# Fifteen of eighteen 128x1024 tiles transposed by a DMA of 16-bit halves instead of matmuls with the identity

## The chip, the cores and the metric

The kernel runs on one core of one Trainium2 chip. The metric is the device time of one execution in microseconds (us), the median of the runs shown. The engines are TensorE (PE), VectorE (DVE), ScalarE (ACT), GpSimd (POOL) and SyncE (SP), which issues all DMAs of this kernel.

## What is computed

An attention block and two feed-forward blocks, on 2304 tokens, in 32-bit floating point. Only the last block is touched by the change:

```python
def _moe2_ref(x, w_in, w_out, g_ln):
    h = x @ w_in                                   # 2304x512 @ 512x1024
    h_max = np.max(h, axis=-1, keepdims=True)
    e = np.exp(h - h_max)
    sm = e / (np.sum(e, axis=-1, keepdims=True) + 1e-09)
    solu = h * sm
    mu = np.mean(solu, axis=-1, keepdims=True)
    var = np.mean((solu - mu) ** 2, axis=-1, keepdims=True)
    ln = (solu - mu) / np.sqrt(var + 1e-06) * g_ln
    return (ln @ w_out).astype(np.float32)         # 2304x1024 @ 1024x512
```

## The kernel before

The kernel is one long program; a scheduler fixes, when it is built, the order of the instructions on each engine. Each engine then works its own queue strictly in that order and waits on semaphores for what other engines and DMAs deliver. Every matmul is done in three passes: an operand is split into a high part (`hi`, L92, a rounding copy on ACT) and a low part (`lo`, L98, a subtraction on DVE), and high x high, high x low and low x high are summed.

The stages before (attention, first feed-forward block, the product of two weight matrices) are left as they are. The last stage runs over 18 tiles of 128 tokens (`NT = 18`, L579) in the loop at L799. One turn of the loop issues, for tile t:

- `h_unit(t)` (L692): 24 matmuls into a PSUM tile `h` of 128x1024; then on DVE a row maximum (L708), on ACT `exp` into `e` (L710), on DVE sum, reciprocal and product into `so` (L711 to L714), the mean (L717), on ACT the squares (L718, written into `e` again), on DVE, POOL and DVE the variance, its power -1/2 and the normalised tile `so` (L719 to L723).
- `x2_unit` (L665), twice with one 128-row part each: 24 matmuls each for the input of the chunk of 256 tokens after this one; each part is evicted and split by ACT and DVE (`x2h`, `x2l`, L94 and L99).
- `tr2(t-1)` (L730): the normalised tile of the turn before, 128 tokens x 1024 features, is turned to features x tokens by 8 matmuls with the identity (L738), into two PSUM tiles; ACT rounds each half into `lh` (L94), DVE subtracts into `ll` (L99).
- `out_unit(t-2)` (L744): 24 matmuls `o` with `lh` and `ll` as stationary operands, an eviction on ACT (L754), and the DMA of 256 KB to the output (L755).
- `split_g` (L652), every second turn: `hi` and `lo` of 8 pieces of the next chunk's input (`gh`, `gl`).

Two lines of pools matter for the change. `e` has a single buffer, and so has the output tile `o`:

```python
e = p2.tile([128, DF], F32, tag="e", bufs=1, name="e")
o = p2.tile([128, DM], F32, tag="o", bufs=1, name="o")
```

`lh`, `ll`, `so` and the PSUM tile `h` have two buffers each.

Of the kernel before, what the change touches and what calls it, by code (L numbers as in the profile page):

```python
# [8 lines left out]
F32 = mybir.dt.float32  # L9
F32R = mybir.dt.float32r  # L10
U32 = mybir.dt.uint32
AF = mybir.ActivationFunctionType
ALU = mybir.AluOpType
AX = mybir.AxisListType
# [11 lines left out]
def tile_attention_moe(  # L26
# [15 lines left out]
    nc = tc.nc  # L42
    B, H, D, _, S = qkT.shape
    NH = B * H
    T, DM = out.shape
    w1, w2, w3L, wo1, w_in, wo2 = (w.bitcast(U32) for w in (w1, w2, w3L, wo1, w_in, wo2))
    DF = w_in.shape[1] // 2
# [38 lines left out]
    def smalltile(name):  # L86
        return PSP[1].tile([128, 512], F32, tag="B", name=name)

    def flat(ap):
        return ap.rearrange("p a b -> p (a b)")  # L90

    def hi(dst, src, eng=None):  # L92
        if eng is None:
            nc.scalar.activation(out=dst, in_=src, func=AF.Copy)  # L94
        else:
            eng.tensor_copy(out=dst, in_=src)

    def lo(dst, src, hi_, eng=nc.vector):  # L98
        eng.tensor_tensor(out=dst, in0=src, in1=hi_.bitcast(F32), op=ALU.subtract)  # L99
# [80 lines left out]
    def softmax_tile(h, ti, ps_in, cut=None):  # L180
# [8 lines left out]
        else:  # L189
# [5 lines left out]
        ex = nc.scalar.activation(  # L195
            out=dst, in_=dst, func=AF.Exp, bias=st[0:rows, ti:ti + 1], scale=-1.0,
            accum_out=st[0:rows, 5 + ti:6 + ti],
# [24 lines left out]
    def normalise(h):  # L222
# [3 lines left out]
        for ti, (q0, rows, n, o) in enumerate(QT):  # L226
            dst = p_t[h][0:rows, o:o + n]
            r = st[0:rows, 10 + ti:11 + ti]
            if ti < 2:
                nc.scalar.activation(out=dst, in_=dst, func=AF.Copy, scale=r)  # L230
            else:
# [83 lines left out]
    def ab_unit(n, f, half):  # L315
# [18 lines left out]
        def a():  # L334
            ps = mm(W1H, W1L, "a")
            a_sb = r0.tile([128, HS], F32, tag="a_sb", bufs=2, name="a_sb")
            nc.scalar.activation(out=a_sb, in_=ps, func=AF.Copy)  # L337
            st["a"] = a_sb
# [18 lines left out]
    def to_f32(raw, eng=nc.gpsimd, dst=None):  # L357

        low, high = raw[:, :, 0], raw[:, :, 1]
        if eng is None:  # L360
            nc.scalar.activation(out=high.bitcast(F32), in_=high.bitcast(F32), func=AF.Copy, scale=2.0 ** -112)
        else:
# [7 lines left out]
        )  # L370
        res = low if dst is None else dst.bitcast(U32)
        nc.vector.scalar_tensor_tensor(
# [23 lines left out]
    def stage(src):  # L396
        raw = stg[0].tile([128, CW, 2], U32, tag="stage", bufs=stg[1], name="stage")
        dst = flat(raw)
        if len(src.shape) == 3:
            dst = dst.rearrange("p (c f) -> p c f", c=src.shape[1])  # L400
        if after[0] is None:
            nc.sync.dma_start(out=dst, in_=src)
        else:
            with tc.issue_after(after[0].ins):
                nc.sync.dma_start(out=dst, in_=src)
        return raw
# [29 lines left out]
    def spill_job(i):  # L436
        src = w_in[i // 2 * 128:i // 2 * 128 + 128, i % 2 * 1024:i % 2 * 1024 + 1024] if i < 8 else wo2[(i - 8) * 128:(i - 7) * 128]

        def conv(raw):
            t = at.tile([128, CW], F32, tag="cst", bufs=2, name="cst")  # L440
            to_f32(raw, None, t)
            if i >= 8:
                nc.scalar.activation(out=t, in_=t, func=AF.Copy, scale=gln[:, i - 8:i - 7])
            nc.sync.dma_start(out=wf_scr[i], in_=t)
# [30 lines left out]
    for i in range(2):  # L475
# [16 lines left out]
        out=wmask[:, S - 128:S], in_=wmask[:, S - 128:S], pattern=[[-1, 128]],  # L492
# [27 lines left out]
    for st, (h, ph) in enumerate(steps):  # L520
# [33 lines left out]
        if h is not None:  # L554
            if h % 2 == 1:
                load_v(h // 2)
            if NQ - 2 <= h < NQ:
                t = QK[h % 2] = at.tile([128, 4, S], F32R, tag="QK", bufs=2, name=f"QK{h % 2}")
# [20 lines left out]
    NT = T // 128  # L579
# [148 lines left out]
    lt_t = {}  # L728

    def tr2(t):  # L730
        so = ln_t.pop(t)
        LH = p2.tile([128, KF, 128], F32R, tag="lh", bufs=2, name="lh")
        LL = p2.tile([128, KF, 128], F32R, tag="ll", bufs=2, name="ll")
        for hf in range(2):
            ps = smalltile("tr2")
            for k in range(4):
                c = hf * 4 + k
                nc.tensor.transpose(ps[:, k * 128:k * 128 + 128], so[:, c * 128:c * 128 + 128], ident)  # L738
            sl = slice(hf * 4, hf * 4 + 4)
            hi(flat(LH[:, sl]), ps)  # L740
            lo(flat(LL[:, sl]), ps, flat(LH[:, sl]))
        lt_t[t] = (LH, LL)

    def out_unit(t):  # L744
        LH, LL = lt_t.pop(t)
        ps = smalltile("o")
        for k in range(KF):
            for l_, w_ in ((LH, OH), (LH, OL), (LL, OH)):
                nc.tensor.matmul(  # L749
                    ps, l_[:, k], w_[:, k],  # L750
                    start=(k == 0 and l_ is LH and w_ is OH), stop=(k == KF - 1 and l_ is LL),
                )
        o = p2.tile([128, DM], F32, tag="o", bufs=1, name="o")
        nc.scalar.activation(out=o, in_=ps, func=AF.Copy)  # L754
        nc.sync.dma_start(out=out[t * 128:t * 128 + 128], in_=o)  # L755
# [32 lines left out]
    p2 = ctx.enter_context(tc.tile_pool(name="p2", bufs=1, side="left"))  # L788
# [10 lines left out]
    for t in range(NT + 2):  # L799
        c, o = divmod(t, 2)  # L800
        if t < NT:
            h_unit(t)
        if t < NT and c + 1 < NCH and 2 * t >= EX:
            x2_unit(c + 1, 2 * o)
        if 0 <= t - 1 < NT - 1:
            tr2(t - 1)
        if t < NT and c + 1 < NCH and 2 * t + 1 >= EX:
            x2_unit(c + 1, 2 * o + 1)
        if t < 2:
            for k in range(4):  # L810
                wf_split(8 + 4 * t + k, V)
        if 0 <= t - 2 < NT:
            out_unit(t - 2)
        if t == NT:
            tr2(t - 1)
        if t < NT and c + 2 < NCH:
            split_g(c + 2, o)
            if o == 1 and c + 3 < NCH:
                load_g(c + 3)
# [50 lines left out]
```

## Time and profile before

| | |
|---|---|
| median of 3 runs (lowest to highest) | 763.17 us (762.51 to 764.19) |
| the profiled execution's own time | 763.22 us |
| its span, first to last instruction | 761.4 us |
| PE busy | 744.4 us (98%), 4864 matmuls |
| PE share of the chain that ended last | 78%, of it the tile transposes (L738) 2% |
| DVE / ACT / POOL busy | 454.9 / 405.9 / 90.6 us |
| mean granted clock of TensorE | 0.995 |

The profile lists busy time per engine over the span, the chain of work that ended last (followed back from the last instruction, each step to what released it), groups of instructions with their mean durations, and waits. In the last stage the names are: `h`, `x`, `o` the three products, `tr` the transposes. The buffer numbers of tiles are left out in the profile's rows.

### The profile page before, as it was taken

How to read it: one execution, taken by the hardware profiler on the slowest of the kernel's cores; microseconds unless marked ns; L12 is line 12 of the kernel's file. 1: busy time of each engine (PE TensorE's matmuls, PEld its weight loads, DVE VectorE, ACT ScalarE, POOL GpSimd, SP SyncE). 2: the span in 40 equal slices, each digit the busy share in tenths (PEclk: the TensorE clock that was granted, in tenths of full speed). 3: DMA queues.
4: the chain of work that ended last, by engine and by line, in shares of the span. 5: the costliest groups of instructions: out<-in, count | busy, mean ns of one | idle time of the engine just before them, and what ended most of it. 6: DMA issues, size and time to landing. Idle time of an engine off the chain costs nothing.

```text
span 761.4 us, 13032 instructions
## 1 busy us (share of the span) xinstructions
PE 744.4 (98%) x4864; PEld 649.6 (85%) x4864; DVE 454.9 (60%) x1165; ACT 405.9 (53%) x927; POOL 90.6 (12%) x93
## 2 busy tenths in 40 slices
PE   8989998999999999999999999999999999999997
PEld 6567978878988988999998898888888888888885
DVE  7877878898777767427868846443435343433341
ACT  4987878898867778415536534332334243222232
POOL 5033313223222121000000000000000000000000
PEclk9999999999999999999999999999999999999999
DMA  4643645566765553106659612221202000000001
GB/s 111 176 121 97 188 134 163 177 171 202 198 173 178 178 161 105 60 32 230 219 163 341 239 56 56 69 53 31 70 15 70 15 15 15 14 15 15 15 28 41
DMA packets 44242, 83.97 MB, mean 110 GB/s; under 512 B 7370, under 2 KB 18634, under 8 KB 44180
## 3 DMA queue, kind: packets, MB, share of 16 engines
q1 hardware_dynamic: 44180, 83.15, 35.8%
q8 instruction: 38, 0.62, 0.3%
q14 instruction: 24, 0.20, 0.1%
HBM read 57.47 MB, written 18.57 MB: 100 GB/s over the span
## 4 chain that ended last, share of the span: by engine, by line
PE 78%; ACT 0%; DVE 0%; issue 0%; ACTq 0%; DVEq 0%
PE o L749 13%; PE x L680 13%; PE h L700 13%; PE b L325 11%; PE a L325 11%; PE m L602 6%; PE av L297 3%; PE tr L264 2%; PE tr L738 2%; PE sc L177 2%; PE sc L178 1%; PE tr L266 0%; PE tr L273 0%; ACT o L754 0%; ACT lh L94 0%; DVE g_sb L345 0%
## 5 line engine op out<-in xcount | busy, mean ns | idle before, releaser
L195 ACT ACTIVATE P<-P,STAT 128x576 f32<-128x576 f32 (+4 forms) x160 | 88.2, 553 | 35.0 <-DVE STAT L191 34.4
L708 DVE TENSOR_REDUCE sv<-h 128x1 f32<-128x1024 f32 x18 | 22.1, 1225 | 119.5 <-PE h L700 119.5
L99 POOL TENSOR_TENSOR QK<-qk,QK 64x1152 fp32r<-64x1152 f32 x24 | 66.5, 2774 | 169.5 <-ACT QK L94 169.3
L680 PE MATMUL x<-gh,MH 128*128 128x256 f32 x288 | 81.7, 284 | 0.0
L680 PE MATMUL x<-gl,MH 128*128 128x256 f32 x288 | 80.5, 279 | 0.0
L680 PE MATMUL x<-gh,ML 128*128 128x256 f32 x288 | 80.4, 279 | 0.0
L191 DVE CUSTOM_DVE_ANT_0 P<-sc,wmask 128x576 f32<-128x576 f32 (+4 forms) x160 | 70.7, 479 | 7.3 <-PE sc L169 5.3
L722 POOL TENSOR_TENSOR sv<-sv,mhalf 128x1 f32<-128x1 f32 x18 | 9.9, 548 | 444.1 <-DVE sv L719 444.1
L325 PE MATMUL b<-xT0h,W 128*128 128x288 f32 x256 | 57.3, 299 | 1.5 <-DVE STAT L191 0.8
L325 PE MATMUL a<-xT0h,W 128*128 128x288 f32 x256 | 57.9, 299 | 0.7 <-ACT a_sb L337 0.7
L749 PE MATMUL o<-OH,lh 128*128 128x512 f32 x144 | 57.1, 397 | 0.3 <-ACT lh L94 0.3
L325 PE MATMUL a<-xT1h,W 128*128 128x288 f32 x256 | 57.2, 298 | 0.0
L749 PE MATMUL o<-OH,ll 128*128 128x512 f32 x144 | 57.0, 396 | 0.0
L749 PE MATMUL o<-OL,lh 128*128 128x512 f32 x144 | 56.8, 395 | 0.0
L700 PE MATMUL h<-IH,x2l 128*128 128x512 f32 x144 | 56.6, 393 | 0.0
L700 PE MATMUL h<-IL,x2h 128*128 128x512 f32 x144 | 56.5, 392 | 0.0
L325 PE MATMUL b<-xT1h,W 128*128 128x288 f32 x256 | 56.5, 294 | 0.0
L700 PE MATMUL h<-IH,x2h 128*128 128x512 f32 x144 | 56.2, 390 | 0.0
L710 ACT ACTIVATE e<-h,sv 128x1024 f32<-128x1024 f32 x18 | 20.1, 1117 | 66.5 <-DVE sv L708 65.1
L680 PEld LDWEIGHTS x<-gl,MH 128*128 128x128 f32 x288 | 54.2, 188 | 1.2
L754 ACT ACTIVATE o<-o 128x512 f32<-128x512 f32 x18 | 10.8, 598 | 83.1 <-PE o L749 83.1
L680 PEld LDWEIGHTS x<-gh,MH 128*128 128x128 f32 x288 | 54.2, 188 | 0.9
(124 smaller groups left out, 1922.4 us busy)
## 6 DMA issues: line engine op xcount, KB each, us to landing
stage<-in_w_dram SPq DMA_DIRECT2D x32, 512.0 KB
g_scr<-g_sb SPq DMA_DIRECT2D x32, 288.0 KB
stage<-in_wo_dram SPq DMA_DIRECT2D x16, 512.0 KB
qk<-in_qk_dram SPq DMA_DIRECT2D x24, 288.0 KB
QK<-QK SPq DMA_DIRECT2D x24, 288.0 KB
graw<-g_scr SPq DMA_DIRECT2D x6, 1024.0 KB
out_dram<-o SPq DMA_DIRECT2D x18, 256.0 KB
VT<-in_vm_dram SPq DMA_DIRECT2D x16, 256.0 KB
```

What stands on the lines that cost most here:

```text
L99: eng.tensor_tensor(out=dst, in0=src, in1=hi_.bitcast(F32), op=ALU.subtract)
L177: nc.tensor.matmul(view, t[:, 0, q0:q0 + rows], t[:, 3, c0:c0 + w], start=True, stop=False)
L191: mx = nc.vector.tensor_tensor_reduce(out=dst2, in0=ps_in, in1=msk, scale=-SCALE, scalar=BIG, op0=ALU.add, op1=ALU.min, accum_out=st[0:row ...
L195: ex = nc.scalar.activation(out=dst, in_=dst, func=AF.Exp, bias=st[0:rows, ti:ti + 1], scale=-1.0, accum_out=st[0:rows, 5 + ti:6 + ti],)
L297: nc.tensor.matmul(st["ps"][64 * e:64 * e + 64, 448 + c0:448 + c1], vr[:, j, e], PT[(2 * p + e) % 4][:, o + c0:o + c1], **kw,)
L325: nc.tensor.matmul(ps, w_[:, c, fs], x_[:, c, sl], start=(c == 0 and w_ is WH and x_ is XH), stop=(c == KC - 1 and w_ is WL),)
L602: nc.tensor.matmul(ps, w_[:, k % 4], o_[:, k], start=(k == 0 and w_ is H3 and o_ is WOH), stop=(k == KF - 1 and w_ is L3),)
L680: nc.tensor.matmul(ps[m], w_[:, k, m * 128:m * 128 + 128], g_[:, k], start=(k == 0 and w_ is MH and g_ is GH), stop=(k == KF - 1 and w_ is ...
L700: nc.tensor.matmul(ps[:, hf], x_[:, k, ts_], w_[:, k, hf * 512:hf * 512 + 512], start=(k == 0 and x_ is XH and w_ is IH), stop=(k == KC - ...
L708: nc.vector.reduce_max(out=sv[:, 0:1], in_=psf, axis=AX.X, negate=True)
L710: nc.scalar.activation(out=e, in_=psf, func=AF.Exp, bias=sv[:, 0:1], scale=1.0, accum_out=sv[:, 1:2])
L749: nc.tensor.matmul(ps, l_[:, k], w_[:, k], start=(k == 0 and l_ is LH and w_ is OH), stop=(k == KF - 1 and l_ is LL),)
```

## The change

For tiles 0 to 14 (`t < NT - 3`), `tr2` uses no matmul. ACT copies the tile, seen as 16-bit halves, so that the 1024 low halves of a row stand first and its 1024 high halves behind (`half`, 128x2048 of 16 bits). One DMA on SP's queue transposes its 16 blocks of 128x128 (`turned`, 512 KB). DVE copies the halves back together (`lt`, 128x1024 of 32 bits). Then `hi` and `lo` make `lh` and `ll` from `lt`, in SBUF, and not from PSUM. `half` takes the one buffer of `e` (`tag="e"`); `turned` and `lt` have one buffer each. Tiles 15 to 17 take the old path.

```diff
+U16 = mybir.dt.uint16
...
         LL = p2.tile([128, KF, 128], F32R, tag="ll", bufs=2, name="ll")
+        if t < NT - 3:
+            half = p2.tile([128, 2, DF], U16, tag="e", bufs=1, name="half")
+            turned = p2.tile([128, 2, DF], U16, tag="turned", bufs=1, name="turned")
+            lt = p2.tile([128, DF], F32, tag="lt", bufs=1, name="lt")
+            nc.scalar.copy(out=half, in_=so.bitcast(U16).rearrange("p (f w) -> p w f", w=2))
+            nc.sync.dma_start_transpose(
+                out=turned.rearrange("p w (k t) -> p (w k) t", t=128), in_=half.rearrange("p w f -> p (w f)"),
+            )
+            nc.vector.tensor_copy(out=lt.bitcast(U16).rearrange("p (f w) -> p w f", w=2), in_=turned)
+            for hf in range(2):
+                sl = slice(hf * 4, hf * 4 + 4)
+                src = lt[:, hf * 512:hf * 512 + 512]
+                hi(flat(LH[:, sl]), src)
+                lo(flat(LL[:, sl]), src, flat(LH[:, sl]))
+            lt_t[t] = (LH, LL)
+            return
         for hf in range(2):
             ps = smalltile("tr2")
```

In the changed file, lines up to L730 of before are one higher, and lines from L734 on are 17 higher: `exp` is L711 there, the eviction of `o` L771, `hi` L95, `lo` L100. The new copy on ACT is L739, the DMA L740, the copy on DVE L743.

The queues up to the last stage are as before. In the last stage they change at these two places.

ACT, before, one turn of the loop for an even tile, past the middle of the stage (`lh<-tr2` is `hi` of the transposed tile, `e<-so` the squares):

```order
L754 ACTIVATE o_6872<-o_6847 128x512
L710 ACTIVATE e_6908,sv_6906<-h_6881,sv_6906 128x1024
L94 ACTIVATE x2h_6775<-x2_6919 128x256
L94 ACTIVATE lh_6946<-tr2_6948 128x512
L94 ACTIVATE lh_6946<-tr2_6955 128x512
L718 ACTIVATE e_6908,sv_6906<-so_6912,sv_6906 128x1024
L94 ACTIVATE x2h_6775<-x2_6962 128x256
```

ACT with the change, in the same part of the stage (`half<-so` is the new copy; `so_7150` is the tile before `so_7286`):

```order
L771 ACTIVATE o_7248<-o_7223 128x512
L95 ACTIVATE lh_7184<-lt_7188 128x512 x2
L711 ACTIVATE e_7282,sv_7280<-h_7255,sv_7280 128x1024
L95 ACTIVATE x2h_7293<-x2_7295 128x256
L719 ACTIVATE e_7282,sv_7280<-so_7286,sv_7280 128x1024
L95 ACTIVATE x2h_7293<-x2_7334 128x256
L739 COPY half_7324<-so_7150 128x2048
L771 ACTIVATE o_7386<-o_7361 128x512
L95 ACTIVATE lh_7322<-lt_7326 128x512 x2
L711 ACTIVATE e_7416,sv_7414<-h_7389,sv_7414 128x1024
```

The two `hi` of a tile stood between `exp` and the squares of the next; now the copy of that tile stands behind the squares and the second `x2h`, and its two `hi` stand in front of the `exp` of the tile after next, which also takes over the buffer that the DMA reads (in turns with `split_g`, four `gh` stand in front of the copy).

DVE, before, the same turns (`ll<-tr` is `lo` of the transposed tile):

```order
L723 TENSOR_SCALAR so<-so,sv 128x1024
L708 TENSOR_REDUCE sv<-h 128x1
L711 TENSOR_SCALAR sv<-sv 128x1
L712 RECIPROCAL sv<-sv 128x1
L714 SCALAR_TENSOR_TENSOR so,sv<-h,sv,e 128x1024
L99 TENSOR_TENSOR x2l<-x_7205,x2h 128x256
L99 TENSOR_TENSOR ll<-tr_7234,lh 128x512
L99 TENSOR_TENSOR ll<-tr_7241,lh 128x512
L717 TENSOR_SCALAR sv<-sv 128x1
```

DVE with the change:

```order
L715 SCALAR_TENSOR_TENSOR so,sv<-h,sv,e 128x1024
L100 TENSOR_TENSOR x2l<-x_7295,x2h 128x256
L718 TENSOR_SCALAR sv<-sv 128x1
L720 TENSOR_SCALAR sv<-sv 128x1
L100 TENSOR_TENSOR x2l<-x_7334,x2h 128x256
L724 TENSOR_SCALAR so<-so,sv 128x1024
L743 COPY lt<-turned 128x2x1024
L100 TENSOR_TENSOR ll<-lt,lh 128x512 x2
L709 TENSOR_REDUCE sv<-h 128x1
```

The two `lo` stood between the product (L714) and the mean (L717); now the joining copy and both `lo` stand in front of the row maximum of the next `h` (in turns with `split_g`, four `gl` stand in front of the joining copy, and the row maximum comes between the two `lo`).

On PE a turn was `h` (24 matmuls, with the 24 of one `x` part, the 8 transposes and the 24 of the other `x` part put in before its last 6) and `o`; it is now `o`, `h`, `x`, `x`. On SP the transposing DMA of a tile stands in front of the output DMA of the tile before.

## Rows read from the trace of the kernel before

**Rows 1.** The page: span, busy time by engine, the chain by engine.

```profile
span 761.4 us, 13032 instructions
PE 744.4 (98%) x4864; PEld 649.6 (85%) x4864; DVE 454.9 (60%) x1165; ACT 405.9 (53%) x927; POOL 90.6 (12%) x93
PE 78%; ACT 0%; DVE 0%; issue 0%; ACTq 0%; DVEq 0%
```

**Rows 2.** Busy time by stretch (length; PE, PEld, DVE, ACT, POOL; clock, DMA share, GB/s).

```profile
600.00:650.00 50.00, 50.00 (x302) 44.26 (x301) 22.28 (x44) 17.93 (x34) 1.64 (x3) 1.00 0.05 17
```

**Rows 3.** The chain in order of time, last stage (start, length, what).

```profile
482.96 0.87 PE tr L738 x8
...
593.53 5.59 PE o L749 x24
599.12 4.13 PE h L700 x18
...
606.07 0.87 PE tr L738 x8
606.94 2.81 PE x L680 x24
609.75 1.38 PE h L700 x6
611.13 5.59 PE o L749 x24
```

**Rows 4.** Timeline of DVE, one turn (start, length, instruction, wait before it).

```profile
603.30 1.23 DVE L708 TENSOR_REDUCE sv<-h 128x1 f32<-128x1024 f32 x1 [8.67 <-PE h L700]
...
606.26 1.28 DVE L714 SCALAR_TENSOR_TENSOR so<-h,sv,e 128x1024 f32<-128x1024 f32 x1
...
607.47 0.42 DVE L99 TENSOR_TENSOR x2l<-x,x2h 128x256 fp32r<-128x256 f32 x1
607.81 1.28 DVE L99 TENSOR_TENSOR ll<-tr,lh 128x512 fp32r<-128x512 f32 x2
609.01 0.15 DVE L717 TENSOR_SCALAR sv<-sv 128x1 f32<-128x1 f32 x1
```

**Rows 5.** Timeline of ACT, the same turn.

```profile
604.64 1.11 ACT L710 ACTIVATE e<-h,sv 128x1024 f32<-128x1024 f32 x1 [4.88 <-DVE sv L708]
...
606.54 1.09 ACT L94 ACTIVATE lh<-tr 128x512 fp32r<-128x512 f32 x2
609.25 1.15 ACT L718 ACTIVATE e<-so,sv 128x1024 f32<-128x1024 f32 x1 [1.62 <-DVE sv L717]
...
610.39 0.36 ACT L94 ACTIVATE x2h<-x 128x256 fp32r<-128x256 f32 x1
610.66 2.18 ACT L94 ACTIVATE gh<-graw 128x512 fp32r<-128x512 f32 x4
```

**Rows 6.** ACT copies in SBUF: tile QK (min/median/max ns); groups by shape, 540 to 720 us.

```profile
L94 ACT ACTIVATE QK<-qk x24: 1160/1164/1176, 46.2 to 287.2; 64x1152 fp32r<-64x1152 f32 x24
...
L94 ACT ACTIVATE gh<-graw 128x512 fp32r<-128x512 f32 x16 | 8.7, 619 | 0.0
```

**Rows 7.** DVE, one source: groups by shape, 540 to 720 us; timeline at 348 us.

```profile
L708 DVE TENSOR_REDUCE sv<-h 128x1 f32<-128x1024 f32 x10 | 12.3, 1225 | 77.1 <-PE h L700 77.1
...
L723 DVE TENSOR_SCALAR so<-so,sv 128x1024 f32<-128x1024 f32 x11 | 8.9, 812 | 2.1 <-POOL sv L722 2.1
...
348.85 0.43 DVE L367 TENSOR_SCALAR stage<-stage 128x512 uint32<-128x512 uint32 x1 [2.73 <-DMA stage<-in_wo_dram]
```

**Rows 8.** The last output DMA: its issue in the timeline, and SP's wait for it.

```profile
758.47 0.33 SPq L755 DMA_DIRECT2D out_dram<-o  x1
...
SPq L865 <- DMA out_dram<-o: 1.6, 1, 1.6
```

**Rows 9.** The page: bytes moved in 40 slices; DMA queue (packets, MB, share of 16 engines).

```profile
GB/s 111 176 121 97 188 134 163 177 171 202 198 173 178 178 161 105 60 32 230 219 163 341 239 56 56 69 53 31 70 15 70 15 15 15 14 15 15 15 28 41
...
q1 hardware_dynamic: 44180, 83.15, 35.8%
```

## The prediction

> **What bounds the kernel now.** I read the page first: PE is busy for 744.4 of 761.4 us, and of the chain that ended last 78% is PE and nearly nothing is any other engine [rows 1]. An average over stages can hide another limit, so next the busy time by stretch: from 600 to 650 us PE has 50.00 of 50 us at full granted clock, DVE 22.28, ACT 17.93, and the DMA engines 5% [rows 2]. Then the chain in order of time: in the last stage it is PE alone, without a gap, and one turn of the loop is six pieces in a row, 593.53 to 611.13, 17.60 us [rows 3]. The 8 transposes of a tile are one of these pieces, 0.87 us, the same from the first to the last. The chain charges only the distance to the next matmul, so 0.87 us is the price on the path; the longer busy time that a group shows overlaps its neighbours and is not to be used.
>
> So every transposed tile taken off PE is worth 0.87 us, as long as PE still gets its operands in time. The question is whether the longer way round through ACT, DMA and DVE stays hidden beneath a turn that is then 17.60 - 0.87 = 16.73 us.
>
> **What is removed.** 15 tiles x 0.87 = 13.05 us of PE. The `hi` and `lo` of the tile remain, at 0.55 us (1.09 for two) and 0.64 us (1.28 for two) each [rows 4, 5]; I take the same from SBUF.
>
> **What is added, per tile.** Three pieces, none of which the trace of before shows.
>
> - The copy `half` on ACT, 2048 elements a row. ACT copies in SBUF took 1.164 us for 1152 elements and 0.619 for 512 [rows 6]: 0.85 ns an element, so 1.164 + 896 x 0.85 ns = 1.93 us. Below it stands 1.11, the `exp` of as many bytes [rows 5]; above it double the slope for the split access, about 3.7. I take 1.93, since the engine's other rows go by elements.
> - The joining copy on DVE, also 2048 elements. One-source work in SBUF took 0.812 us for 1024 and 0.43 for 512 [rows 7]: 0.75 ns an element, so 0.812 + 1024 x 0.75 ns = 1.58, taken as 1.6. Bounds: 0.81 (as many bytes) and 2.45 (twice the row maximum's 1.225, the slowest rate in the stage).
> - The DMA, D. The output DMA of 256 KB landed 0.33 + 1.6 = 1.9 us after SP began to issue it [rows 8]. 512 KB take 0.77 us more at the best slice's 341 GB/s [rows 9]: 2.7 us is the lower bound. Two such DMAs one after the other would be 3.9. The far bound: a row of a 128-wide block of 16-bit elements is 256 bytes, 2048 such pieces, 128 for each of 16 engines; the kernel's mean packet costs 0.358 x 16 x 761.4 us / 44180 = 99 ns [rows 1, 9], so 12.6 us of packets behind a start of about 1.2 (1.9 less the data's 0.77): 13.8 us. That mean is over packets of 1.9 KB, so the value belongs near the lower end; I take 3.5.
>
> As pure load this fits: 3.5 us more on ACT and DVE together for each turn, against 27.7 and 32.1 us idle in 50 [rows 2]; the DMA queue is nearly empty here. PSUM traffic falls.
>
> **The round that the new order closes.** What decides is not load but a ring of waits. With the change DVE takes the row maximum of tile n+1 only behind the joining copy and `lo` of tile n-1, and ACT takes `exp` of n+1 behind the two `hi` of n-1 and only once the DMA has read `half`, because both share one buffer. The DMA of n-1 in turn waits for `half`, which stands behind the squares of tile n. So one round leads from row maximum to row maximum, and its length must be under a PE turn. From the timelines, counted from 603.30 [rows 4, 5]:
>
> - row maximum to the end of the product: 606.26 + 1.28 - 603.30 = 4.24; `x2l` ends at 607.89, 4.59. Before, the two `lo` came here (607.81 to 609.01); now the mean follows directly, 0.15, and the squares 0.24 after its start: 4.83. From the squares to the second `x2h` is 610.39 - 609.25 = 1.14, and 0.27 more until ACT is free: 6.24 us.
> - in every second turn four `gh`, 2.18.
> - `half` 1.93, DMA 3.5, join 1.6, one `hi` 0.55, one `lo` 0.64, and a second `lo`, 0.64, in turns without `gh`; five handoffs between engines at 0.1 (the row maximum ends at 604.53, `exp` starts at 604.64), 0.5.
>
> Without `gh`: 6.24 + 1.93 + 3.5 + 1.6 + 0.55 + 1.28 + 0.5 = 15.60. With `gh`: 6.24 + 2.18 + 1.93 + 3.5 + 1.6 + 0.55 + 0.64 + 0.5 = 17.14. Mean 16.37, against 16.73 of PE: 0.36 us to spare. A single late turn is caught by PE's own slack: the last `x2l` is wanted only after the next `o`, some 4 us later than it is ready. Write S for the sum of the three new pieces, 7.03 here. Up to S = 7.4 PE never waits; beyond it each round is longer by S - 7.4, in about 14 rounds (tiles 1 to 14).
>
> For `o` the way is free too: tile n-1 is complete about 15 us after the row maximum of n began, and its `o` stands behind two `x`, one `o`, one `h` and two more `x`, 22 us. On SP each transposing DMA waits for its `half`; behind it stands an output DMA whose data comes later anyway, so that costs nothing. The tail (tiles 15 to 17) keeps its order: nothing.
>
> **Sum.** The profiled execution took 763.22 us, the median is 763.17, the same. 763.2 - 13.05 = 750.2 us.
>
> **The rivals.**
>
> 1. *The forecast:* S at most 7.4, all 13.05 us gained, 750.2. For it: all three middle estimates. Against it: the margin is 0.4 us on three prices that no row shows. Chance 0.55.
> 2. *Part of it is given back:* S between 7.4 and 8.2, for instance a join at 2.45, S = 7.88, a loss of 14 x 0.48 = 6.7 us: 756.9. Chance 0.19. The no-change strip around S = 8.33 (13.05 / 14 = 0.93 over 7.4) gets 0.04.
> 3. *Slower: the ring becomes the bound.* Place: the row maximum on DVE and `exp` on ACT wait for the transposing DMA of the tile before the last. The point that decides is S = 8.33, that is D = 4.8 with the other two as taken. At D = 6, S = 9.53 and the loss 14 x 2.13 = 29.8: 780 us. For it: the far bound of the DMA lies well beyond, and the loss is steep, 14 us for each us. Against it: the output DMA's 1.9 us. Chance 0.20, of it 0.07 up to D = 5.5 (14 x 1.63 = 22.8, 773).
> 4. *The 16 blocks go one after another:* if each paid a DMA's start of 1.2 us, D = 16 x 1.2 + 1.5 of data = 20.7, S = 24.2, a loss of 14 x 16.8 = 235: 985 us. Chance 0.02. Against it: 256 KB in 128 rows did not pay any such thing in the output DMA [rows 8]. Beside it, the Trainium skill's page "VectorE: DVE Perf Modes", section "The three transpose paths", gives 1309 ns for a 128x128 transpose of 16-bit elements by DMA against 390 ns on TensorE, and advises TensorE when the result may go to PSUM. By that price, paid 16 times in a row, the sum would come to some 989 us. No run here shows a transposing DMA yet.
>
> That the change does not do what it says is excluded by the order of the instructions: 15 transposing DMAs stand on SP, and three groups of 8 transposes are left on PE.
>
> **Range and chances.** About 0.2%, 1.5 us, is what a measurement of this kernel can tell from no change. From 749 (the forecast with its spread) to 773 (D = 5.5) the cases hold 0.55 + 0.19 + 0.04 + 0.07 = 0.85; the rest lies above. Faster 0.55 + 0.19 = 0.74, same 0.04, slower 0.22. The forecast's own range is 749 to 752.
>
> **What would show it.** Right: a turn of 16.7 us in the chain, `o`, `h`, `x`, `x` without gaps, PE still about 50 of 50 us between 600 and 650, `half` near 1.9 us, the join near 1.6, and the join starting about 3.5 us after `half` ends. Wrong: gaps on PE before `h` or `o`; DVE idle in front of the join with the DMA as releaser, for over 5 us, and `exp` waiting likewise; then the turn equals the ring and not PE's work. If the turn is 16.7 us and the time is still not near 750, the loss lies at the start or the end of the stage, which I cost at nothing.

## The result and the profile after

| | before | after |
|---|---|---|
| median (lowest to highest) | 763.68 us (762.51 to 764.78, 4 runs) | 751.07 us (750.47 to 753.42, 4 runs) |
| ratio to before, 95% interval | | 0.9841 [0.9814, 0.9868] |
| profiled execution, its span | 763.22, 761.4 us | 750.76, 749.0 us |

The kernel is faster by 12.6 us, against a forecast of 13.05. The page of the kernel after answers to [rows 1, 9]: PE lost 120 matmuls and 13.6 us of busy time, DVE gained 20.6 us and ACT 26.4 us, and the DMA moved 31,200 packets more, all of them under 512 bytes (38,570 now, 7,370 before). The last row is the new joining copy. In the chain by engine 10% are now DMA, of it 4% the transposing one and 4% a load of an earlier stage.

```profile
PE 730.8 (98%) x4744; PEld 636.1 (85%) x4744; DVE 475.5 (63%) x1180; ACT 432.3 (58%) x942; POOL 90.6 (12%) x93
DMA packets 75441, 91.82 MB, mean 123 GB/s; under 512 B 38570, under 2 KB 49834, under 8 KB 75380
PE 72%; DMA 10%; DVE 10%; ACT 5%; issue 1%; POOL 1%; ACTq 0%; SPq 0%; DVEq 0%; POOLq 0%
L743 DVE COPY lt<-turned 128x2048 uint16<-128x2048 uint16 x15 | 20.2, 1344 | 60.5 <-DMA turned<-half 60.5
```

Busy time by stretch answers to [rows 2] (length; PE, PEld, DVE, ACT, POOL; clock, DMA share, GB/s). From 600 us on PE is as full as before. In the two stretches ahead of that it is not: 0.76 and 0.15 us are idle.

```profile
500.00:550.00 50.00, 49.24 (x276) 42.16 (x276) 24.70 (x46) 22.72 (x37) 1.65 (x3) 1.00 0.37 95
550.00:600.00 50.00, 49.85 (x286) 43.38 (x285) 26.24 (x46) 23.26 (x37) 1.65 (x3) 1.00 0.27 69
600.00:650.00 50.00, 50.00 (x289) 43.80 (x289) 26.72 (x49) 24.62 (x41) 1.65 (x3) 1.00 0.18 48
```

The chain in order of time, late in the stage, answers to [rows 3]. From `o` to `o` a turn is 652.62 - 635.94 = 16.68 us (16.73 was forecast), without a gap.

```profile
635.94 5.59 PE o L766 x24
641.52 5.50 PE h L701 x24
647.02 5.60 PE x L681 x48
652.62 5.59 PE o L766 x24
```

The new pieces can be read from the timelines of the same turn, that of ACT here and that of DVE below it (start, length, instruction, wait before it). The copy `half` takes 1.89 us and ends at 640.56. The joining copy starts at 644.38, and its releaser is the DMA: 3.82 us from the end of one to the start of the other. The join takes 1.33 us. One `hi` and one `lo` from SBUF take 0.62 and 0.69 us, nearly as from PSUM before (0.60 and 0.68).

```profile
638.67 1.89 ACT L739 COPY half<-so 128x2048 uint16<-128x2048 uint16 x1
```

The timeline of DVE, the same turn:

```profile
644.38 1.33 DVE L743 COPY lt<-turned 128x2048 uint16<-128x2048 uint16 x1 [3.82 <-DMA turned<-half]
```

What was not foreseen stands early in the stage. There the chain runs through the transposing DMA, which takes twice as long in some tiles:

```profile
493.24 5.33 DMA turned<-half
...
508.83 6.87 DMA turned<-half
...
524.98 3.68 DMA turned<-half
...
542.61 7.46 DMA turned<-half
...
550.10 1.37 DVE lt L743
...
551.49 0.64 ACT lh L95
```

SP's timeline shows what sets the long ones of 6.9 to 7.5 us apart. In these, SP has issued the load of the next chunk's input (`graw`, up to 1 MB) right in front of the transposing DMA, and then is held for some 5 us by the latter instead of 1.6. The load waits until the last `gl` has read its buffer, the transposing DMA until `half` is written, and with `split_g` in the turn both happen at once: here the last `gl` ends at 542.11 and `half` at 542.12 us.

```profile
542.13 0.37 SPq L645 DMA_DIRECT2D graw<-g_scr  x1
542.61 5.44 SPq L740 DMA_TRANSPOSE turned<-half  x1
...
558.00 1.57 SPq L740 DMA_TRANSPOSE turned<-half  x1
```

The one of 5.33 us at 493.24 has no load in front. While it ran, only one packet of 0.02 MB on the instruction queue moved beside it; whether that held it up was not tested.

From 500 to 720 us the waits (total, times, longest) show who pays. `exp` waits twice for the DMA, up to 7.7 us, because `half` lies in `e`'s buffer. `lh` is late three times at `o`, and `ll` once:

```profile
ACT e L711 <- DMA turned<-half: 15.3, 2, 7.7
...
PEld o L766 <- ACT lh L95: 1.3, 3, 0.7
PEld o L766 <- DVE ll L100: 0.7, 1, 0.7
```

These are three late `o`, at 500.93, 517.80 and 552.17 us. In the first, the `exp` that waited for the DMA of 493.24 stands in front of `lh` on ACT. In the other two `lh` waits for the join, and the join for a DMA with a load in front, as the last lines of the chain above show. What a late `o` costs is read from the starts of the matmuls in PE's timeline, which are 0.12 us apart in `x` and 0.23 in `h` and `o`. At the third it is 0.43 instead of 0.12:

```profile
551.74 0.28 PE L681 MATMUL x<-gh,ML 128*128 128x256 f32 x1
552.17 0.50 PE L766 MATMUL o<-OH,lh 128*128 128x512 f32 x1
```

The next start, at 552.51, is again 0.11 late. Summed in this way the three cost 0.63, 0.94 and 0.42 us, 2.0 in all; PE's idle time shows only about half of it.

A measure for the stage alone is needed, since its first `h` starts between 451.5 and 456.6 us in the profiled executions below, though no queue differs up to there. From the first `h` to the end of the span the stage took 761.4 - 453.1 = 308.3 us before and 749.0 - 451.9 = 297.1 after: 11.2 us less.

### The profile page after: what moved, and what is told of

Its sections match the earlier page's. It is cut to its first block, busy times and chain, and to the rows that moved or that the text cites. A ratio compares the mean times of both kernels' runs of the same rounds, so it can differ in the third digit from the quotient of the medians.

```text
span 749.0 us, 12853 instructions
## 1 busy us (share of the span) xinstructions
PE 730.8 (98%) x4744; PEld 636.1 (85%) x4744; DVE 475.5 (63%) x1180; ACT 432.3 (58%) x942; POOL 90.6 (12%) x93
## 2 busy tenths in 40 slices
DMA packets 75441, 91.82 MB, mean 123 GB/s; under 512 B 38570, under 2 KB 49834, under 8 KB 75380
## 4 chain that ended last, share of the span: by engine, by line
PE 72%; DMA 10%; DVE 10%; ACT 5%; issue 1%; POOL 1%; ACTq 0%; SPq 0%; DVEq 0%; POOLq 0%
PE o L766 11%; PE h L701 10%; PE x L681 10%; PE a L326 9%; PE b L326 9%; PE m L603 6%; PE av L298 6%; DMA stage<-in_w_dram 4%; DMA turned<-half 4%; PE tr L265 4%; PE sc L178 2%; PE sc L170 2%; PE sc L179 2%; DVE P L192 1%; ACT P L196 1%
## 5 line engine op out<-in xcount | busy, mean ns | idle before, releaser
L100 POOL TENSOR_TENSOR QK<-qk,QK 64x1152 fp32r<-64x1152 f32 x24 | 66.6, 2776 | 169.6 <-ACT QK L95 169.4
L743 DVE COPY lt<-turned 128x2048 uint16<-128x2048 uint16 x15 | 20.2, 1344 | 60.5 <-DMA turned<-half 60.5
L681 PEld LDWEIGHTS x<-gh,ML 128*128 128x128 f32 x288 | 54.1, 188 | 0.3
L362 ACT ACTIVATE stage<-stage 128x512 f32<-128x512 f32 x56 | 37.8, 681 | 23.9 <-DMA stage<-in_w_dram 16.4
```

The costliest lines, as they stand in the source:

```text
L681: nc.tensor.matmul(ps[m], w_[:, k, m * 128:m * 128 + 128], g_[:, k], start=(k == 0 and w_ is MH and g_ is GH), stop=(k == KF - 1 and w_ is ...
L743: nc.vector.tensor_copy(out=lt.bitcast(U16).rearrange("p (f w) -> p w f", w=2), in_=turned)
```

## The experiments

The theory: the matmuls give 13 us, the longer way round hides beneath PE's turn as long as S is under about 7.4 us, and some 2 us are lost early, where the transposing DMA stands behind a load on SP and `exp` waits for its buffer. The rivals: nothing is lost, or the loss lies in the way round itself; a longer way would cost nothing at all; the loss comes from something else at the start.

### e1: nothing in the place of the transposes

For tiles 0 to 14 the transposition is left out; `hi` and `lo` read `so` directly.

```diff
-            half = ...; turned = ...; lt = ...
-            nc.scalar.copy(out=half, ...)
-            nc.sync.dma_start_transpose(out=turned..., in_=half...)
-            nc.vector.tensor_copy(out=lt..., in_=turned)
...
-                src = lt[:, hf * 512:hf * 512 + 512]
+                src = so[:, hf * 512:hf * 512 + 512]
```

> Leaves the transposition of tiles 0 to 14 out altogether: high and low parts are made straight from the untransposed tile, without the copy to halves, the DMA, the joining copy or any matmul with the identity. Theory (PE's queue is the bound, the way through ACT, DMA and DVE is hidden beneath it): the same time as with the change, 750.2 to 751.1 us, and the changed kernel is at most some 0.7 us above it. Rival (the DMA way still holds PE up, and part of the gain is lost): this one is 2 us or more below the changed kernel, 749 or less.

748.78 us (748.12 to 750.02), ratio 0.9816 [0.9792, 0.984]: 2.3 us below the change. The intervals of the two ratios overlap, so the times alone do not settle it. The stage does: 746.3 - 451.5 = 294.8 us, 13.5 less than before, with PE 50.00 of 50 us in every stretch from 450 to 700. So the change could give 13.5 us and gives 11.2. The row of the `h` matmuls puts the missing time between the first and the last of them (minimum/median/maximum ns, first and last start). First after:

```profile
L701 PE MATMUL h<-IH,x2l x144: 387/389/398, 452.7 to 725.3; 128*128 128x512 f32 x144
```

and e1, 270.5 us where after has 272.6:

```profile
L701 PE MATMUL h<-IH,x2l x144: 387/389/398, 452.3 to 722.8; 128*128 128x512 f32 x144
```

### e2: only every other tile by DMA

```diff
-        if t < NT - 3:
+        if t < NT - 3 and t % 2 == 0:
```

> Only the 8 even ones of tiles 0 to 14 go by DMA, the other 7 and the last 3 by matmuls. Theory (0.87 us of PE for each tile): 763.7 - 8 x 0.87 = 756.7 us. Rival (the gain comes from something that is not per tile, such as the two products of 24 matmuls now standing together on PE, or PSUM tiles that come free): near 763 or near 751, not half way.

755.74 us (754.45 to 759.84), ratio 0.9902 [0.9873, 0.993]. Eight of the fifteen tiles are off PE, and the gain is 7.7 us: 0.96 a tile, with an interval of 5.3 to 9.7 us that holds 8 x 0.87 = 7.0. The stage is 757.8 - 456.6 = 301.2 us, 7.1 less than before. PE has 50.00 of 50 us in every stretch from 450 to 700, although SP is held for 5.4 to 5.6 us by three of the eight transposing DMAs, each behind a load: a late DMA alone does not cost PE anything here. The chain has both kinds of turn side by side. From `h` to `h` it is 17.55 us with the transposes (614.50 to 632.05), and from `o` to `o` 16.69 us without (626.46 to 643.15), a difference of 0.86:

```profile
614.50 5.49 PE h L701 x24
...
622.79 0.87 PE tr L755 x8
...
626.46 5.59 PE o L766 x24
632.05 5.49 PE h L701 x24
...
643.15 5.59 PE o L766 x24
```

### e3 and e4: the DMA twice

In both the DMA is issued twice in a row. In e3 the row maximum of a tile is also held behind the last `lo` issued before it, so that the scheduler cannot loosen the ring; in e4 it is free.

```diff
+            nc.sync.dma_start_transpose(out=turned..., in_=half...)
...
+            with tc.issue_after(ring[0].ins):   # e3 alone; ring[0]: the last lo
                 nc.vector.reduce_max(out=sv[:, 0:1], in_=psf, axis=AX.X, negate=True)
```

> The transposing DMA is issued twice in a row per tile, the second waiting for the first, and the row maximum of a tile is kept in the queue behind the low part of the transposed tile before, so that the ring of waits stands as in the changed kernel. The trace of the changed kernel gives 1.89 us for the copy, 1.34 for the join and 3.7 for the DMA. Theory (ring, 14 us for each us beyond a sum of 7.4): the sum is 1.89 + 1.34 + 7.4 = 10.6, a loss of 14 x 3.2 = 45 us against 751, so 796 us, a turn of about 20 us and DVE waiting for the DMA before each join. Rival (PE has far more room than the ring tells, since buffers are double): under 765 us. Second rival (the second DMA finds everything ready and takes under 2 us): about 775.

> The same doubled DMA, but the scheduler is left free: it now puts the exp of a tile in front of the high parts of the one two before, and the joining copy behind the next row maximum. Theory (the ring, not the DMA's length by itself, sets the loss; the exp still waits for the buffer that the DMA reads): well under the 796 of the forced order, 757 to 775. Rival (the DMA's length is paid wherever it stands): the same time as with the forced order.

e3: 790.27 us (788.45 to 792.84), ratio 1.036 [1.0329, 1.0392], slower than before. Its chain runs through both transfers of each tile, and the first starts 655.08 - 636.72 = 18.36 us after the last tile's:

```profile
636.72 3.64 DMA turned<-half
640.38 3.67 DMA turned<-half
...
655.08 3.76 DMA turned<-half
```

So each DMA costs 3.65 us. PE has gaps in every turn, 45.5 to 47.1 busy of 50 us from 500 to 750, since the tile comes late to `o`, as in rival 3 of the prediction; DVE waits 12 times for the DMA, up to 8.0 us (from 450 to 760 us):

```profile
PEld o L773 <- ACT lh L95: 32.2, 15, 6.5
```

Thirteen turns, from one `half` at 501.30 to that at 746.94, average 18.9 us. The formula of the prediction gives 16.73 + (10.55 - 7.4) = 19.9. The scheduler had put both `x2h` and the `gh` behind `half`, out of the ring, which the formula does not have.

e4: 759.25 us (756.2 to 764.16), ratio 0.9943 [0.9919, 0.9968]. The same second DMA costs 8 us instead of 39 when the scheduler may place the row maximum and `exp`: the ring is a property of an order and not of the work.

### e5, e6 and e8: the two links of the early loss

e5 puts the load of the next chunk behind the transposing DMA on SP. e6 gives `half` the buffer of `lt` instead of that of `e`, so `exp` need not wait for the DMA. e8 has both edits.

```diff
+            turn[0] = nc.sync.dma_start_transpose(...)          # e5, e8
...
+                with tc.issue_after(turn[0].ins):               # e5, e8
                     load_g(c + 3)
...
-            half = p2.tile([128, 2, DF], U16, tag="e", ...)
+            half = p2.tile([128, 2, DF], U16, tag="lt", ...)    # e6, e8
```

> The load of the next chunk's input (up to 1 MB, its buffer comes free at the same moment as the copy to halves ends) is issued behind the transposing DMA of the turn, not in front of it. In the changed kernel's trace a transposing DMA landed 3.7 us after its issue, but some 7 us when that load had been issued just before. Theory (the 2.3 us by which the changed kernel stands above the one without any turning are lost early in the stage, where these slow DMAs lengthen the ring): all transposing DMAs near 3.7 us, and 749 to 750.3 us. Rival (the loss comes from the order at the start of the stage, not from the meeting of two DMAs): 751 as with the change. Second rival (the load now comes too late and the split of the input waits for it): above 751.5.

> The halves no longer take the buffer of e, but share one with the joined tile, so exp need not wait until the DMA has read them; DVE's order is the scheduler's. Theory (the shared buffer holds exp up only where a DMA is slow, 22 us of waiting in 4 turns, most of it covered by PE's queue): 749.5 to 751. Rival (the shared buffer is what closes the ring, and without it all is gained): equal to the kernel without turning, 748.8. Second rival (halves and joined tile in one buffer make a new wait, the copy to halves behind the low part of the tile before): above 751.5.

> Both: the load behind the transposing DMA, and the halves not in e's buffer. Theory: no transposing DMA above 4 us and no exp waiting for one; within 0.7 us of the kernel without any turning, 748.8 to 749.5. Rival (the two edits mend the same waits): equal to the better of the two alone. Second rival (the scheduler's new order costs more than the waits did): above 751.

| | median (lowest to highest) | ratio, interval | stage |
|---|---|---|---|
| e5 | 749.21 (748.2 to 753.08) | 0.9822 [0.98, 0.9843] | 294.8 |
| e6 | 750.42 (748.04 to 751.07) | 0.9822 [0.9804, 0.984] | 294.7 |
| e8 | 749.14 (748.2 to 751.78) | 0.981 [0.9796, 0.9825] | 294.7 |

By the times none of these can be told from the change or from another, since the intervals overlap. In the profiles all three have the stage length of e1, and PE 50.00 of 50 us from 450 to 700. In e5 SP's timeline shows short DMAs only, with the load behind them:

```profile
536.58 1.41 SPq L741 DMA_TRANSPOSE turned<-half  x1
538.04 0.59 SPq L645 DMA_DIRECT2D graw<-g_scr  x1
```

In e6 the load still stands in front and SP still holds 5.4 us, yet PE does not wait:

```profile
541.94 0.38 SPq L645 DMA_DIRECT2D graw<-g_scr  x1
542.41 5.41 SPq L740 DMA_TRANSPOSE turned<-half  x1
```

So either edit gives the 2.3 us back. That the loss needs both links, the late DMA and the buffer that it keeps from `exp`, is not shown by this, because neither build changes one link alone. In both the scheduler has also ordered the early matmuls otherwise: from about 500 us on they run as whole `o`, `h`, `x`, `x`, where the kernel after still puts two matmuls of an `o` ahead of most of an `h` up to 586. And in e6 SP issues the load within 0.5 us in front of a transposing DMA at two places, 541.94 and 574.66, where the kernel after has four.

### e7: all eighteen tiles by DMA

```diff
-        if t < NT - 3:
+        if t < NT:
```

> All 18 tiles go by DMA. Theory (a tile is only free while other matmuls cover its way; the last ones have just one or two products of 24 matmuls behind them): 3 x 0.87 = 2.6 us of PE fewer, but after the last h PE waits for copy, DMA, join, high and low part, about 8 us, less than the 0.87 and the wait of before: 753 to 760 us. Rival (gain per tile everywhere): 751.1 - 2.6 = 748.5.

759.15 us (757.34 to 759.58), ratio 0.9938 [0.9922, 0.9953], 8 us above the change, although PE has three more tiles less to turn. At the end nothing is left that could cover the way round. The chain leaves PE when the last `h` ends (724.80) and comes back at 740.41; the pieces between are the layer norm, which every version has there, and the new way; its DMA is shown:

```profile
733.70 3.64 DMA turned<-half
...
740.41 13.27 PE o L766 x48
```

Part of the 8 us is clock. PE does nothing from 724.8 to 728.0 and has a second gap up to 729.8; busy time by stretch gives a granted clock of 0.56 and 0.58 from 728 on, and it is low again behind the gap that ends at 740.41. In all, 19 matmuls of `o` start 0.43 us apart instead of 0.23, at the lower of the clock's two levels, and none in the kernel after: 19 x 0.20 = 3.8 us, an estimate from these starts.

```profile
728.00:732.00 4.00, 3.03 (x7) 2.11 (x8) 2.56 (x6) 1.93 (x4) 0.00 (x0) 0.56 0.02 4
732.00:736.00 4.00, 4.00 (x12) 3.10 (x12) 0.81 (x1) 1.68 (x1) 0.55 (x1) 0.58 0.33 76
```

### e9: the DMA in two

```diff
+            for w in range(2):
+                nc.sync.dma_start_transpose(
+                    out=turned[:, w].rearrange("p (k t) -> p k t", t=128), in_=half[:, w],
+                )
```

> The transposing DMA is split in two of 256 KB, one for each half of the values. If its 3.7 us are mostly data, the second lands about 3.7 to 4 us after the first is issued and the time stays at 751 us (750 to 753). If they are mostly a price per transfer, the second lands about 7 us after the first is issued, S = 1.9 + 7 + 1.3 = 10.2 us; by the ring of the prediction (threshold 7.4) that would cost 14 x 2.8 = 39 us, 790 us, and with the exponentials and row maxima as free to move as in e4 some 757 to 765 us.

750.43 us (748.78 to 752.41), ratio 0.9833 [0.9801, 0.9865]; stage 748.2 - 453.4 = 294.8. In the turn that answers to the one shown of after, `half` ends at 640.07 and the join starts at 644.30 (DVE's timeline), 4.23 us where one transfer needs 3.82. The second transfer thus adds 0.4 us, and not another 3.65, though SP needs 2.60 us to issue the two, where one takes 1.6. In the kernel after, no packet moves from the issue at 558.00 to 559.1, and all 2080 do from there to 561.3: some 2 of the 3.7 us go with the bytes, which are the same in e9, and the second transfer is issued while the first is under way.

```profile
644.30 1.34 DVE L744 COPY lt<-turned 128x2048 uint16<-128x2048 uint16 x1 [4.23 <-DMA turned<-half]
```

This run also narrows the account of the early loss. `graw` is still in front (541.66 on SP), `exp` still waits for the DMA three times (up to 7.4 us), and PE has no gap. In the turn of the first gap the scheduler has put three more matmuls of `h` in front of the `o`. In the other two turns the order is nearly that of the kernel after, but `lh` starts 2.4 and 2.0 us sooner, counted from the first `h` (516.19 and 550.95 less 453.4, against 517.12 and 551.49 less 451.9). A late DMA and a held buffer are therefore not enough for the loss: it takes a tile that comes some tenths of a us after PE has run out of other work.

### e10: the join twice, with the ring held as in e3

```diff
+            nc.vector.tensor_copy(out=lt.bitcast(U16)..., in_=turned)
...
+            with tc.issue_after(ring[0].ins):
                 nc.vector.reduce_max(out=sv[:, 0:1], in_=psf, axis=AX.X, negate=True)
```

> The join is done twice and the row maximum of a tile is held behind the last rest of the tile before, as in e3, so the ring of the prediction cannot be loosened: S = 1.9 + 3.7 + 2 x 1.34 = 8.3 us. By the prediction's threshold (S = 7.4) the stage loses 14 x 0.9 = 12 us, 763 us, as much as the matmuls gave. By what e3 showed (turns of 18.4 us at S = 9.3 + 0.0 with half a copy less in the ring), a ring of 18.4 - 3.7 + 1.3 = 16.1 us stays under TensorE's 16.7 and the time is 751 to 753 us.

767.91 us (766.8 to 769.11), ratio 1.0059 [1.0036, 1.0082]: slower than before. The starts of `half` in ACT's timeline give the turns, here 17.72 and 16.07 us:

```profile
603.84 1.90 ACT L743 COPY half<-so 128x2048 uint16<-128x2048 uint16 x1
...
621.56 1.90 ACT L743 COPY half<-so 128x2048 uint16<-128x2048 uint16 x1
...
637.63 1.91 ACT L743 COPY half<-so 128x2048 uint16<-128x2048 uint16 x1
```

DVE's timeline tells the two kinds apart: in the long ones pieces of `gl` stand between the two joining copies, which then start 3.04 us apart instead of 1.38, and 16.07 + 1.66 = 17.73.

```profile
609.43 1.35 DVE L747 COPY lt<-turned 128x2048 uint16<-128x2048 uint16 x1 [0.30 <-DMA turned<-half]
610.67 1.89 DVE L100 TENSOR_TENSOR gl<-graw,gh 128x512 fp32r<-128x512 f32 x3
612.47 1.32 DVE L748 COPY lt<-turned 128x2048 uint16<-128x2048 uint16 x1
...
627.14 1.34 DVE L747 COPY lt<-turned 128x2048 uint16<-128x2048 uint16 x1 [0.28 <-DMA turned<-half]
628.52 1.34 DVE L748 COPY lt<-turned 128x2048 uint16<-128x2048 uint16 x1
```

My second expectation (16.1 us in every turn, so no loss) held only for turns without `gl`; I had left `gl` out of the ring. The prediction's threshold, S = 8.27 against 7.4, asked for 763 and is the nearer of the two. The 13 turns from 498.38 to 722.65 average 17.25 us, 0.56 over PE's 16.69 where the formula had 0.87: 7.3 us in all. The stage is 766.1 - 454.1 = 312.0 us, 17.2 more than e1's, so 10 us more were lost. Half of that shows in the first turn (20.58 us from `half` to `half`, against 15.71 in after), and the trace points to a cause: SP has issued a load in front of the first transposing DMA. `half` ends at 477.80 + 1.89 = 479.69, and in DVE's timeline the first join starts 8.04 us later:

```profile
487.73 1.34 DVE L747 COPY lt<-turned 128x2048 uint16<-128x2048 uint16 x1 [3.78 <-DMA turned<-half]
```

That is 4.2 more than the 3.8 of a transfer alone. In the kernel after the same wait is as long (477.49 to 485.44) and the turn is not, since there the row maximum does not stand behind the tile. What is left shows behind the last `h`, where PE meets the tiles that the turns have made late: it has gaps from 728.2 to 731.6 and from 738.6 to 741.2 and runs at a lower clock behind each. Counted on PE alone, by the starts of its matmuls, 8.2 of the 17.2 us are lost ahead of the last `h` and 9.0 behind it.

## Why the prediction was right

- **The 13.05 us of PE.** Right. A turn went from 17.60 to 16.68 us (0.92 less), the difference of the two kinds side by side in e2 is 0.86, and without them and with nothing in their place the stage is 13.5 us shorter (e1).
- **The three prices.** `half` 1.89 (1.93 taken), join 1.34 (1.6), DMA about 3.7 (3.5), S = 6.9 where 7.03 was taken. The nearest rows were the right ones: the rate by elements for both copies, and the output DMA for the transposing one. The far bound of 13.8 us, from the kernel's mean packet, was far off: 2048 pieces of 256 bytes went through in 3.65 us.
- **The ring.** Right in kind: with S at 8.27 (e10) and 10.55 (e3) PE waits for the tile before, the turn equals the ring, and the kernel is slower than before, as rival 3 had it. In size the formula is too long by 0.35 us a turn in e10 (17.25 measured, 17.6) and by 1.0 in e3 (18.9, 19.9), where `x2h` and `gh` had left the ring. Wrong as a law: the loss of 14 us for each us beyond the threshold holds for one order, and with the order free the same DMA twice cost 8 us (e4). The price of rival 3 was therefore too high for a scheduled kernel.
- **The step that failed.** "On SP each transposing DMA waits for its `half`; behind it stands an output DMA whose data comes later anyway, so that costs nothing." That looks at what stands behind the transposing DMA and not at what stands in front of it: the load of the next chunk. In those tiles D was 6.9 to 7.5 us, S over 10. PE's own slack took most of it, and 2.3 us of 13.5 stayed lost, at "the start or the end of the stage, which I cost at nothing", as the prediction's last sentence allowed. Which link makes a late DMA a loss (the buffer of `e`, or the order of the matmuls) stays open: e5 and e6 changed both. That the time of 751.07 lies only 0.9 above the forecast is in part luck. The stage gained 11.2 us and not 13.05; 1.2 of the 12.4 us between the two profiled executions lie ahead of the stage (453.1 and 451.9), where no queue differs. And e1 shows 0.45 more to gain than 13.05.
- **Rivals 2 and 4** fell. The join was quicker than estimated. For rival 4, the 16 blocks of one DMA took 3.65 us together, 0.23 us a block. The Trainium skill's page "VectorE: DVE Perf Modes", section "The three transpose paths", gives 1309 ns for one block by DMA, and its section "Rules for kernel authors" advises TensorE when the result may go to PSUM. The trace does not bear out that price once 16 blocks share a transfer, and in a kernel whose chain is PE alone the slower path is the cheaper one.

## What to carry to other kernels

When a matmul is replaced by a longer way over other engines, price it by the round that the new waits close (from an instruction on its engine, through the way, back to the same instruction one tile on), and compare that with a turn of the bound engine: under it the way is free, above it every turn pays as long as the order holds (e3), and much less where the scheduler may change the order (e4). Then look on the queue of each new DMA at what is issued just in front of it, above all loads that are released by the same moment; here ordering one load behind, or giving the DMA's source a buffer that the next tile does not need, brought PE's gaps to nothing, each with a new order of the matmuls beside it. And leave the last tiles on the short way, since nothing covers them: 8 us here (e7), about half of it by the clock that falls behind the gaps.

The quickest versions by their medians are e8 (749.14) and e5 (749.21). Their profiles show the 2.3 us of the early loss gone; a time below that of the change is not shown by their intervals.

## What the runs showed that I had not expected

- A DMA behind a load on one queue: 3.7 us alone, 6.9 to 7.5 us with a load just issued. An estimate from the rows: 1 MB at the 343 GB/s of the best slice of the page after is 3.1 us, and 3.1 + 3.7 = 6.8. The transposing DMA would then have waited for the load's bytes, and the packets of the one issued at 542.61 bear this out. From 542 to 547.2 only packets of 512 bytes and more move, those of the load, and 2096 smaller ones follow from 547.2 to 550. That these DMAs are short without a load in front is shown by e5; the sum is an estimate.

```profile
DMA packets 928, 0.95 MB, mean 183 GB/s; under 512 B 0, under 2 KB 928, under 8 KB 928
```

- Gaps on PE can cost clock as well, in e7 and here. In e10, by stretch, PE has little to do from 728 to 732, and the granted clock is 0.60 in the stretch behind it, where it is busy throughout; the `o` matmuls there start 0.43 us apart, and 0.23 later, which are the two levels of the clock, 1.2 and 2.4 GHz.

```profile
728.00:732.00 4.00, 0.88 (x6) 0.57 (x5) 3.04 (x3) 1.08 (x3) 0.00 (x0) 0.98 0.01 2
732.00:736.00 4.00, 4.00 (x12) 2.98 (x11) 4.00 (x6) 2.24 (x5) 0.00 (x0) 0.60 0.02 4
```
